# A gated filter and an MLP in fp32: the second MLP product with the weights held and a transposed output, and 97 instead of 98 positions in half of the tiles

## Chip, cores and metric

The kernel runs on one NeuronCore of one Trainium2 chip. The metric is the device time of one execution in microseconds (us). A NeuronCore has a matrix engine (TensorE, PE in the profile, with its weight loads as a row of their own, PEld), a vector engine (VectorE, DVE), a scalar engine (ScalarE, ACT), a general engine (GpSimd, POOL) and a queue engine that here only issues transfers (SyncE, SP). Each runs its own instructions in order and waits on semaphores for the others.

## What is computed

```python
def _attn_ref(x, v, pos_emb, w1, w2):            # B, S, D = 2, 12480, 128
    h_filt = (np.maximum(pos_emb @ w1, 0.0) @ w2) * np.exp(-0.01 * np.arange(S))[:, None]
    u = x * v
    L = 2 * S
    Uf = np.fft.rfft(u, n=L, axis=1)
    Hf = np.fft.rfft(h_filt, n=L, axis=0)
    y = np.fft.irfft(Uf * Hf[None, :, :], n=L, axis=1)[:, :S, :]
    return x * y

def _moe_ref(x, w_in, w_out, a, b):              # x: 24960 x 128, w_in: 128 x 2048, w_out: 2048 x 128
    h = x @ w_in
    P = a[0] + a[1] * h + a[2] * h**2 + a[3] * h**3
    Q = 1.0 + abs(b[0]) * abs(h) + abs(b[1]) * h**2
    return (P / (Q + 1e-06)) @ w_out
```

A long convolution along the sequence, a gate with x, and then an MLP with a rational activation, all in fp32.

## The kernel before

The sequence of 12480 positions is written as a grid: position = 128 m + n, with n the residue (0 to 127) and m the row (0 to 97). Residues 0 to 63 have 98 real rows, residues 64 to 127 only 97. The convolution is a Fourier transform over this grid, made of matrix products.

A first part (some 370 us) computes the filter's spectrum and the convolution of batch 0. A second part (`second_part`, taken in its `short` form) does the rest: the last Fourier step of both batches by tile (`attn_a`, `attn_b`), the MLP of every tile, and, spread between, the convolution of batch 1 (`conv_items`).

The MLP goes by 52 tiles. A tile is 5 residues of one batch (every 13th one has 4), so 5 x 98 = 490 columns (or 392) with the 128 channels on the partitions. Tiles 0 to 12 and 26 to 38 are residues from 64 up, tiles 13 to 25 and 39 to 51 residues below 64; before the change both have 98 positions a residue, the 98th of the former being a filler that isn't stored. The hidden 2048 features are done in 4 steps a tile, 4 blocks of 128 features each, so there are 208 steps. A step has two halves of two blocks:

- `mm1`: h = features x columns into PSUM, three fp32r passes a block (L870 to L872), `[128, 2, 490]` a half.
- ACT, DVE and POOL turn h into g, kept as four rows of 490 columns a step in tiles `q` and `v`: ACT writes `q` (L880, L887), `v` (L904), squares (L932, L937), takes the logarithm `l` of all four rows at once (L948) and the exponential `r` (L953); DVE does L914, L959, L964 (and L893); POOL does L969 and, last, the product `v <- v * q` (L975). A cost per row and column is so paid some 20 times a step on ACT.
- `mm2`: the second product, from `v` and `wout`, into the PSUM tile `acc`; a half is two blocks. After the 16th block `store` copies `acc` out (DVE) and SP issues the transfers.

The order of the work on each engine is written out by two strings: `FIRST` for the steps up to 94, `REST` from step 95 on. In `FIRST` each of the three slots of a step (`slot`) also issues an item of batch 1's convolution or a part of the next tile's last Fourier step, which share the one PSUM tile `cv`; in some steps POOL also multiplies a loaded piece of x and v (`uq`, L245). In `REST` the convolution is over. The order isn't touched by the change. SP issues the loads and the stores in one queue.

Of the kernel before, what the change touches and what calls it, by code (L numbers as in the profile page):

```python
# [9 lines left out]
F32 = mybir.dt.float32  # L10
# [100 lines left out]
def build(ctx: ExitStack, tc, x, x_q, v_q, pos_emb, w1, w2, w_in, w_out, moe_a, moe_b,  # L111
# [534 lines left out]
    def second_part(short):  # L646
# [142 lines left out]

        def load_xg(j):  # L790
# [36 lines left out]
        def attn_b(j):  # L827
            n = tiles[j][2]
            w = n * M
# [3 lines left out]
            def fill(cv):  # L833
                for i in range(n):
                    nc.tensor.transpose(out=cv[:, 0, i * M:(i + 1) * M], in_=t[:, i, :], identity=ident[0:M, 0:M])
# [17 lines left out]
        def width(s):  # L853
            return tiles[steps[s][0]][2] * M
# [7 lines left out]
        def mm1(s, i):  # L862
            j, c = steps[s]
            w = width(s)
            hi, lo = ah[j]
# [7 lines left out]
            st_h[s, i] = t[:, :, 0:w]  # L873
# [103 lines left out]
        def mm2(s, h):  # L977
            j, c = steps[s]
            w = width(s)
            if j not in acc:  # L980
                acc[j] = accp.tile([128, 4, D], F32, tag="acc", name="acc")
            g = st_v[s]
            for i in range(2 * h, 2 * h + 2):
                f = NWF * c + i
                for q in range(0, w, 128):
                    k = min(128, w - q)
                    nc.tensor.matmul(out=acc[j][0:k, q // 128, :], lhsT=g[:, i, q:q + k], rhs=wout[:, f, :],  # L987
                                     start=(f == 0 and q == 0), stop=(f == NF - 1), skip_group_check=True)

        def store(j):  # L990
            b, p0, n = tiles[j]
            n0 = residue(p0, n)
            w = n * M
            t = mp.tile([128, 4, D], F32, tag="ot", name="ot", bufs=2)
            a = acc.pop(j)
            nq = (w + 127) // 128
            full = w // 128
            nc.vector.tensor_copy(out=t[:, 0:full, :], in_=a[:, 0:full, :])
            if full < nq:
                k = w - full * 128  # L1000
                nc.vector.tensor_copy(out=t[0:k, full, :], in_=a[0:k, full, :])
            ob = out[b * S:(b + 1) * S, :]
            p = 0
            while p < w:
                i, m = divmod(p, M)
                k = min(M - m, 128 - p % 128)
                mm = min(k, (M if n0 + i < H2 else M - 1) - m)
                if mm > 0:
                    nc.sync.dma_start(out=ob[bass.DynSlice(m * N2 + n0 + i, mm, step=N2), :],
                                      in_=t[p % 128:p % 128 + mm, p // 128, :])  # L1010
                p += k
# [63 lines left out]
_OUTS = [((B * S, D), "float32")]  # L1075
# [30 lines left out]
```

## Time and profile before

| | |
|---|---|
| median of 3 runs | 2253.34 us (2252.31 to 2254.02) |
| profiled execution, own time | 2255.12 us |
| its span, first to last instruction | 2253.2 us |
| PE busy | 2023.2 us (90%), 13344 matmuls |
| DVE busy | 2073.7 us (92%), 2374 instructions |
| ACT busy | 1941.2 us (86%), 1971 instructions |
| POOL busy | 2021.5 us (90%), 1605 instructions |
| chain that ended last, by engine | ACT 41%, POOL 22%, PE 22%, DVE 7%, issue 5%, DMA 2% |

Busy times are averages over a first part, in which ACT has little to do, and a second part, in which four engines are nearly full. The rows of single stretches say more than the table. "The chain" is followed back from the last instruction, at each step to what released it.

### The profile page before, as it was taken

What the parts mean: (1) busy time and instruction counts of PE and PEld (TensorE: products, weight loads), DVE (VectorE), ACT (ScalarE), POOL (GpSimd) and SP (SyncE); (2) the same over time, 40 slices, a digit from 0 to 9 for tenths busy, and PEclk for the clock granted to TensorE, in tenths of its full rate; (3) what the DMA queues carried; (4) which work ended last, traced back from release to release, by engine and by line L of the source; (5) the groups of instructions that cost most, each with busy time, mean ns of one, the idle gap of its engine ahead of it and who ended that gap; (6) DMA issues with size and microseconds to landing.
All of it is one profiled execution on the core that took longest, in us unless ns stands there. A gap on an engine that the chain in (4) does not pass through costs nothing.

```text
span 2253.2 us, 35705 instructions
## 1 busy us (share of the span) xinstructions
PE 2023.2 (90%) x13344; PEld 1758.5 (78%) x13344; DVE 2073.7 (92%) x2374; ACT 1941.2 (86%) x1971; POOL 2021.5 (90%) x1605
## 2 busy tenths in 40 slices
PE   6899987899999999999999889888888898888887
PEld 4678775788888888888888777777777777777775
DVE  6899995899998998999999789999999999999996
ACT  5422224999999998999999899999999999999996
POOL 5488765999999999999999789999999999999997
PEclk9999998999999999999999999999999999999999
DMA  5344415433143233223222212212112111221100
GB/s 159 107 142 143 130 62 146 106 94 81 36 117 80 51 87 83 70 60 76 58 62 52 49 33 46 48 34 46 31 36 49 38 40 33 48 48 33 36 10 11
DMA packets 169487, 150.31 MB, mean 67 GB/s; under 512 B 91622, under 2 KB 138984, under 8 KB 166424
## 3 DMA queue, kind: packets, MB, share of 16 engines
q1 hardware_dynamic: 162280, 124.17, 22.5%
q10 hardware_dynamic: 7024, 23.76, 3.2%
q8 instruction: 107, 1.75, 0.3%
q14 instruction: 76, 0.62, 0.1%
HBM read 99.72 MB, written 48.17 MB: 66 GB/s over the span
## 4 chain that ended last, share of the span: by engine, by line
ACT 41%; POOL 22%; PE 22%; DVE 7%; issue 5%; DMA 2%; SPq 1%; POOLq 0%; DVEq 0%; ACTq 0%
POOL v L975 10%; ACT v L904 10%; ACT l L948 9%; ACT r L953 9%; PE acc L987 5%; POOL v L969 4%; ACT q L880 4%; ACT q L937 4%; ACT q L932 3%; PE cs L155 3%; PE cs L582 2%; POOL q L943 2%; PE cv L816 2%; PE h L870 1%; PE h L872 1%
## 5 line engine op out<-in xcount | busy, mean ns | idle before, releaser
L975 POOL TENSOR_TENSOR v<-v,q 128x980 f32<-128x980 f32 (+1 forms) x416 | 940.6, 2262 | 52.0 <-DVE q L964 48.7
L987 PE MATMUL acc<-wout,v 128*128 128x128 f32 (+2 forms) x6656 | 846.2, 280 | 112.4 <-POOL v L975 108.0
L987 PEld LDWEIGHTS acc<-wout,v 128*128 128x128 f32 (+2 forms) x6656 | 776.6, 187 | 191.5 <-POOL v L975 165.8
L959 DVE SCALAR_TENSOR_TENSOR q<-q,sc,r 128x980 f32<-128x980 f32 (+1 forms) x416 | 504.6, 1213 | 36.3 <-ACT r L953 34.9
L914 DVE SCALAR_TENSOR_TENSOR v<-v,sc,h 128x980 f32<-128x980 f32 (+1 forms) x416 | 504.7, 1213 | 35.4 <-ACT q L880 30.4
L964 DVE SCALAR_TENSOR_TENSOR q<-q,r 128x980 f32<-128x980 f32 (+1 forms) x416 | 482.0, 1159 | 13.5
L904 ACT ACTIVATE v<-h,sc 128x980 f32<-128x980 f32 (+1 forms) x416 | 438.1, 1082 | 30.9 <-PE h L872 29.4
L953 ACT ACTIVATE r<-l 128x980 f32<-128x980 f32 (+1 forms) x416 | 416.8, 1002 | 9.8 <-DVE q L964 8.9
L969 POOL TENSOR_SCALAR v<-v,sc 128x980 f32<-128x980 f32 (+3 forms) x321 | 422.3, 1316 | 0.0
L948 ACT ACTIVATE l<-q,sc 128x1960 f32<-128x1960 f32 (+1 forms) x208 | 401.1, 1928 | 0.7 <-POOL q L943 0.5
L870 PE MATMUL h<-ahi,win_l 128*128 128x490 f32 (+1 forms) x832 | 360.9, 434 | 28.6 <-DVE v L914 26.6
L871 PE MATMUL h<-alo,win_h 128*128 128x490 f32 (+1 forms) x832 | 319.6, 384 | 0.0
L872 PE MATMUL h<-ahi,win_h 128*128 128x490 f32 (+1 forms) x832 | 317.6, 382 | 0.0
L880 ACT ACTIVATE q<-h 128x980 f32<-128x980 f32 (+1 forms) x303 | 302.5, 998 | 8.9 <-PE h L872 8.8
L870 PEld LDWEIGHTS h<-ahi,win_l 128*128 128x128 f32 x832 | 158.6, 191 | 60.5 <-DVE v L914 38.4
L932 ACT ACTIVATE q<-q,sc 128x1960 f32<-128x1960 f32 (+1 forms) x95 | 185.9, 1957 | 0.0
L872 PEld LDWEIGHTS h<-ahi,win_h 128*128 128x128 f32 x832 | 158.0, 190 | 26.0
L937 ACT ACTIVATE q<-q,sc 128x1470 f32<-128x1470 f32 (+1 forms) x113 | 170.6, 1510 | 0.0
L871 PEld LDWEIGHTS h<-alo,win_h 128*128 128x128 f32 x832 | 159.2, 191 | 13.5 <-DVE alo L841 0.4
L816 PE MATMUL cv<-yc,gt 90*98 90x128 f32 x1004 | 127.9, 274 | 2.2 <-DVE an L822 1.0
L816 PEld LDWEIGHTS cv<-yc,gt 90*98 90x98 f32 x1004 | 118.3, 165 | 14.1 <-DVE an L822 7.5
L943 POOL TENSOR_TENSOR q<-q 128x490 f32<-128x490 f32 (+1 forms) x113 | 111.4, 986 | 9.4
(113 smaller groups left out, 2623.5 us busy)
## 6 DMA issues: line engine op xcount, KB each, us to landing
yc<-y_d SPq DMA_DIRECT2D x23, 900.0 KB
gt<-in_g_dram SPq DMA_DIRECT2D x48, 344.5 KB
xq<-in_x_q_dram SPq DMA_DIRECT2D x64, 196.0 KB
vq<-in_v_q_dram SPq DMA_DIRECT2D x64, 196.0 KB
h_d<-hg ACTq DMA_DIRECT2D x32, 360.0 KB
y_d<-ys ACTq DMA_DIRECT2D x16, 720.0 KB
hg<-h_d SPq DMA_DIRECT2D x64, 180.0 KB
y_d<-ys SPq DMA_DIRECT2D x16, 720.0 KB
```

Source lines behind the costliest of these rows:

```text
L870: nc.tensor.matmul(out=t[:, k, 0:w], lhsT=wl, rhs=hi[:, 0:w], start=True, stop=False)
L871: nc.tensor.matmul(out=t[:, k, 0:w], lhsT=wh, rhs=lo[:, 0:w], start=False, stop=False)
L872: nc.tensor.matmul(out=t[:, k, 0:w], lhsT=wh, rhs=hi[:, 0:w], start=False, stop=True)
L904: nc.scalar.activation(out=v, in_=st_h[s, i], func=AF.Square, bias=col("s"))
L914: stt(out=v, in0=v, scalar=col("k"), in1=h, op0=ALU.add, op1=ALU.mult)
L948: nc.scalar.activation(out=part(st_l, s, i), in_=part(st_q, s, i), func=AF.Ln, **({"bias": col("ka")} if short else {}))
L953: nc.scalar.activation(out=t[:, :, 0:w], in_=halves(st_l[s], i, w), func=AF.Exp, scale=-1.0)
L959: nc.vector.scalar_tensor_tensor(out=q, in0=q, scalar=col("ka") if short else 0.0, in1=st_r[s, i], op0=ALU.add, op1=ALU.mult)
L964: nc.vector.scalar_tensor_tensor(out=q, in0=q, scalar=2.0, in1=st_r.pop((s, i)), op0=ALU.subtract, op1=ALU.mult)
L969: nc.gpsimd.tensor_scalar(out=v, in0=v, scalar1=col("p0" if short else "a0"), scalar2=1.0, op0=ALU.add, op1=ALU.mult)
L975: nc.gpsimd.tensor_tensor(out=v, in0=v, in1=halves(st_q[s], i, w), op=ALU.mult)
L987: nc.tensor.matmul(out=acc[j][0:k, q // 128, :], lhsT=g[:, i, q:q + k], rhs=wout[:, f, :], start=(f == 0 and q == 0), stop=(f == NF - 1), ...
```

## The change

Three things are changed. `mm2` swaps its operands: the block of `wout` is loaded into the array as the weights and the columns of `v` stream through, one matmul a block of 485 to 490 (or 388 to 392) columns, where before pieces of 128 columns of `v` were loaded as weights and the 128 columns of `wout` streamed, four matmuls a block. `acc` is so `[channel, column]`, is copied out by one DVE instruction, and one transfer a tile writes it to an output that is laid out by channel; the host turns it round afterwards. And tiles of residues from 64 up have 97 positions a residue (`count`), so 485 or 388 columns; where fp32r matmuls or the high and low split need an even number, one more column is carried along (486).

```diff
+        def count(j):
+            return M if tiles[j][1] >= H2 else M - 1
...
         def attn_b(j):
             n = tiles[j][2]
-            w = n * M
+            k1 = count(j)
+            w = n * k1 + n * k1 % 2
...
                 for i in range(n):
-                    nc.tensor.transpose(out=cv[:, 0, i * M:(i + 1) * M], in_=t[:, i, :], identity=ident[0:M, 0:M])
+                    k = min(M, w - i * k1) if i == n - 1 else k1
+                    nc.tensor.transpose(out=cv[:, 0, i * k1:i * k1 + k], in_=t[0:k, i, :], identity=ident[0:k, 0:k])
...
         def width(s):
-            return tiles[steps[s][0]][2] * M
+            j = steps[s][0]
+            return tiles[j][2] * count(j)
...
         def mm1(s, i):
             w = width(s)
+            w += w % 2
...
         def mm2(s, h):
             if j not in acc:
-                acc[j] = accp.tile([128, 4, D], F32, tag="acc", name="acc")
-            g = st_v[s]
+                acc[j] = accp.tile([D, 512], F32, tag="acc", name="acc")
             for i in range(2 * h, 2 * h + 2):
                 f = NWF * c + i
-                for q in range(0, w, 128):
-                    k = min(128, w - q)
-                    nc.tensor.matmul(out=acc[j][0:k, q // 128, :], lhsT=g[:, i, q:q + k], rhs=wout[:, f, :],
-                                     start=(f == 0 and q == 0), stop=(f == NF - 1), skip_group_check=True)
+                nc.tensor.matmul(out=acc[j][:, 0:w], lhsT=wout[:, f, :], rhs=st_v[s][:, i, 0:w],
+                                 start=(f == 0), stop=(f == NF - 1), skip_group_check=True)

         def store(j):
-            t = mp.tile([128, 4, D], F32, tag="ot", name="ot", bufs=2)
-            nc.vector.tensor_copy(out=t[:, 0:full, :], in_=a[:, 0:full, :])
-            if full < nq:
-                nc.vector.tensor_copy(out=t[0:k, full, :], in_=a[0:k, full, :])
-            while p < w:
...
-                    nc.sync.dma_start(out=ob[bass.DynSlice(m * N2 + n0 + i, mm, step=N2), :],
-                                      in_=t[p % 128:p % 128 + mm, p // 128, :])
+            w = n * count(j)
+            t = mp.tile([D, NPT * M], F32, tag="ot", name="ot", bufs=2)
+            nc.vector.tensor_copy(out=t[:, 0:w], in_=acc.pop(j)[:, 0:w])
+            r0 = n0 * M - max(0, n0 - H2)
+            nc.sync.dma_start(out=out[b, :, r0:r0 + w], in_=t[:, 0:w])
```

On PE, in the last `FIRST` step that begins before the 4-residue tile of batch 0, a half of the second product (`acc`) stands between a convolution item (L215) and the next (L155), with the first product of the 4-residue tile (`h`, 128x392) behind. The sizes are partitions x columns of what is written. Before:

```order
L215 MATMUL cv<-idfth,yy 90x2x64 x4
L987 MATMUL acc<-wout,v 128x128 x3
L987 MATMUL acc<-wout,v 106x128
L987 MATMUL acc<-wout,v 128x128 x3
L987 MATMUL acc<-wout,v 106x128
L155 MATMUL cv<-f_66,uq_5084 128x180 x2
L870 MATMUL h<-ahi,win_l 128x392
```

And at the same place after the change:

```order
L215 MATMUL cv<-idfth,yy 90x2x64 x4
L992 MATMUL acc<-v,wout 128x485 x2
L155 MATMUL cv<-f_66,uq_4774 128x180 x2
L878 MATMUL h<-ahi,win_l 128x388
L879 MATMUL h<-alo,win_h 128x388
```

Eight matmuls with 128 streamed columns each have become two with 485; nothing was moved past anything else.

On SP, the store of a tile stands between the loads for a later tile (`xt`, `gt`, `yc`) and those of the convolution (`hg`). Before:

```order
L143 DMA xt<-in_x_dram 96x640
L146 DMA xt<-in_x_dram 2x640
L797 DMA gt<-in_g_dram 90x980
L779 DMA yc<-y_d_64 90x32x80
L1009 DMA out_dram<-ot 97x128
L1009 DMA out_dram<-ot 30x128
L1009 DMA out_dram<-ot 67x128
L1009 DMA out_dram<-ot 60x128
L1009 DMA out_dram<-ot 37x128
L1009 DMA out_dram<-ot 90x128
L1009 DMA out_dram<-ot 7x128
```

And after:

```order
L146 DMA xt<-in_x_dram 2x640
L801 DMA gt<-in_g_dram 90x980
L779 DMA yc<-y_d_64 90x32x80
L1002 DMA out_dram<-ot 128x485
L703 DMA hg<-h_d 128x2x180
L692 DMA y_d_65<-ys 90x2048
```

Eight transfers (an eighth row, 97x128, follows those shown) have become one, in the same place of the queue.

## Rows read from the trace of the kernel before

**Rows 1.** Busy time by stretch: us, then PE, PEld, DVE, ACT, POOL, granted clock, DMA.
```profile
600.00:800.00 200.00, 190.55 (x1355) 174.84 (x1353) 186.16 (x186) 197.25 (x182) 194.98 (x164) 1.00 0.32 78
2000.00:2200.00 200.00, 173.91 (x1179) 150.03 (x1179) 195.94 (x204) 199.85 (x192) 198.00 (x143) 1.00 0.14 31
```

**Rows 2.** Waits of ACT, 420 to 2253 us: total, times, longest.
```profile
ACT v L904 <- PE h L872: 18.3, 19, 3.7
```

**Rows 3.** Timeline, two FIRST steps: start, duration, engine, line.
```profile
717.78 1.96 ACT L948 ACTIVATE l<-q,sc 128x1960 f32<-128x1960 f32 x1
...
727.37 1.98 ACT L948 ACTIVATE l<-q,sc 128x1960 f32<-128x1960 f32 x1
...
735.36 0.38 PE L872 MATMUL h<-ahi,win_h 128*128 128x490 f32 x1
...
735.78 1.08 ACT L904 ACTIVATE v<-h,sc 128x980 f32<-128x980 f32 x1
...
736.75 1.93 ACT L948 ACTIVATE l<-q,sc 128x1960 f32<-128x1960 f32 x1
```

**Rows 4.** Timeline of ACT, a FIRST step without a convolution item on ACT.
```profile
803.70 1.99 ACT L948 ACTIVATE l<-q,sc 128x1960 f32<-128x1960 f32 x1
...
812.81 2.01 ACT L948 ACTIVATE l<-q,sc 128x1960 f32<-128x1960 f32 x1
```

**Rows 5.** Groups by form: tiles of 5 and of 4 residues (count, busy, mean ns).
```profile
L975 POOL TENSOR_TENSOR v<-v,q 128x980 f32<-128x980 f32 x384 | 880.8, 2295 | 45.0 <-DVE q L964 41.7 <-ACT q L932 3.1
...
L948 ACT ACTIVATE l<-q,sc 128x1960 f32<-128x1960 f32 x192 | 375.3, 1955 | 0.2
...
L975 POOL TENSOR_TENSOR v<-v,q 128x784 f32<-128x784 f32 x32 | 59.8, 1868 | 7.0 <-DVE q L964 7.0
...
L948 ACT ACTIVATE l<-q,sc 128x1568 f32<-128x1568 f32 x16 | 25.8, 1612 | 0.5 <-POOL q L943 0.5
```

**Rows 6.** The chain, 726 to 734 us: start, time on the chain, what.
```profile
726.12 1.77 PE acc L987 x16
...
733.20 0.31 PE cv L190 x2
...
```

**Rows 7.** Timeline of PE and its weight loads, first product.
```profile
729.27 0.38 PE L871 MATMUL h<-alo,win_h 128*128 128x490 f32 x1
729.49 0.38 PE L872 MATMUL h<-ahi,win_h 128*128 128x490 f32 x1
```
**Rows 8.** Timeline of the weight loads alone, same stretch.
```profile
729.27 0.19 PEld L872 LDWEIGHTS h<-ahi,win_h 128*128 128x128 f32 x1
```

**Rows 9.** The chain in REST: POOL's second product of a step, twice.
```profile
1704.72 2.27 POOL v L975
...
1713.10 2.28 POOL v L975
```

**Rows 10.** Timeline of ACT in REST, start of the l of steps 107 and 108.
```profile
1400.37 1.97 ACT L948 ACTIVATE l<-q,sc 128x1960 f32<-128x1960 f32 x1
1408.66 2.00 ACT L948 ACTIVATE l<-q,sc 128x1960 f32<-128x1960 f32 x1
```

**Rows 11.** Timeline of ACT, l of a tile of 4 residues (steps 152 and 155).
```profile
1776.61 1.61 ACT L948 ACTIVATE l<-q,sc 128x1568 f32<-128x1568 f32 x1 [0.18 <-POOL q L943]
...
1801.02 1.60 ACT L948 ACTIVATE l<-q,sc 128x1568 f32<-128x1568 f32 x1
```

**Rows 12.** The chain in the same stretch.
```profile
1789.95 2.16 PE acc L987 x16
```

**Rows 13.** Timeline of POOL after the 4-residue tile of batch 0 in FIRST.
```profile
889.02 2.30 POOL L975 TENSOR_TENSOR v<-v,q 128x980 f32<-128x980 f32 x1 [2.01 <-ACT q L932]
```

**Rows 14.** Timeline of the end of the kernel.
```profile
2242.63 2.43 PE L987 MATMUL acc<-wout,v 128*128 128x128 f32 x16 [0.56 <-POOL v L975]
2245.10 0.56 DVE L998 COPY ot<-acc 128x384 f32<-128x384 f32 x1 [4.51 <-PE acc L987]
2245.68 3.44 SPq L1009 DMA_DIRECT2D out_dram<-ot  x7
```

More of the change, by code (lines that the diff above doesn't have):

```diff
@@ L872, in mm1 @@
                 nc.tensor.matmul(out=t[:, k, 0:w], lhsT=wh, rhs=hi[:, 0:w], start=False, stop=True)
-            st_h[s, i] = t[:, :, 0:w]
+            st_h[s, i] = t[:, :, 0:width(s)]
         def act_q(s, i):
@@ L992, in store @@
             n0 = residue(p0, n)
-            w = n * M
-            t = mp.tile([128, 4, D], F32, tag="ot", name="ot", bufs=2)
-            a = acc.pop(j)
-            nq = (w + 127) // 128
-            full = w // 128
-            nc.vector.tensor_copy(out=t[:, 0:full, :], in_=a[:, 0:full, :])
-            if full < nq:
-                k = w - full * 128
-                nc.vector.tensor_copy(out=t[0:k, full, :], in_=a[0:k, full, :])
-            ob = out[b * S:(b + 1) * S, :]
-            p = 0
-            while p < w:
[L1005 to L1008, printed above, removed]
-                    nc.sync.dma_start(out=ob[bass.DynSlice(m * N2 + n0 + i, mm, step=N2), :],
-                                      in_=t[p % 128:p % 128 + mm, p // 128, :])
-                p += k
+            w = n * count(j)
[3 more added lines that the diff above has]
+            nc.sync.dma_start(out=out[b, :, r0:r0 + w], in_=t[:, 0:w])
         at = []
@@ L1074, with by_position @@
 _INS = ["x", "v", "pos_emb", "w1", "w2", "moe_w_in", "moe_w_out", "moe_a", "moe_b"]
-_OUTS = [((B * S, D), "float32")]
+_OUTS = [((B, D, S), "float32")]
+def by_position(a):
+    a = a.reshape(B, D, S).transpose(0, 2, 1)
+    r = np.empty((B, S, D), np.float32)
+    o = 0
+    for n in range(N2):
+        k = M if n < H2 else M - 1
+        r[:, n::N2] = a[:, o:o + k]
+        o += k
+    return r.reshape(B * S, D)
 def by_quarter(x):
@@ L1104 @@
     r = _run(nc, [arrays], core_ids=[0])
-    return r.results[0]["out_0_dram"]
+    return by_position(np.asarray(r.results[0]["out_0_dram"]))
```

## The prediction

> **What bounds the kernel now.** I read the busy time by stretch first. The second part has two stretches: while the convolution of batch 1 runs (`FIRST`) ACT is busy 197.25 of 200 us, PE 190.55 and POOL 194.98; after it (`REST`) ACT 199.85, POOL 198.00, DVE 195.94, and PE only 173.91, always with the full granted clock [rows 1]. So PE isn't what limits most of the time, and a cheaper second product is worth only what it frees the others from. Then the starts of ACT's `l`, which comes once a step: 9.59 us apart in a `FIRST` step with a convolution item on ACT, 9.11 us in one without, and between two starts ACT's instructions follow each other without a gap [rows 3, 4]. But of the 95 steps up to the switch, 14 that have no such item take 9.36 to 9.41 us; one of them is 727.37 to 736.75, in which ACT's `v` at 735.78 begins when the first product's last pass has just ended (735.36 plus 0.38) [rows 3]. There PE is late by 9.38 - 9.11 = 0.27 us, and the chain of what ended last runs over PE for 12 us ahead of it, with two halves of the second product in it [rows 6]. In all ACT's `v` waits 18.3 us for the first product, 19 times that the list counts [rows 2]. In `REST` the chain goes round in POOL (a second product `v * q` every 8.38 us) or in ACT (8.29 us), two loops that are equal within 1% [rows 9, 10].
>
> **The second product.** Before, a half takes 1.77 us on the chain: 16 records, two for each of 8 matmuls of 128 streamed columns, so 0.111 us a record [rows 6]. What streaming 485 columns costs is bounded by the same kind of matmul with 180 columns: two records in 0.31 us, 0.155 each, that is 0.86 ns a column [rows 6]; from the two sizes, (0.155 - 0.111) / 52 gives 0.85 ns a column and next to nothing fixed. A record of 485 columns is then 0.41 us, a half (four records) 1.63 to 1.65 us, with 490 columns 1.65 to 1.67, with 388 or 392 1.32 to 1.34. I take 0.13 us a half off, since 512 streamed columns become 485 to 490 and nothing else is saved. In a tile of 4 residues a half took 2.16 us on the chain [rows 12] (its last piece of 8 columns is streamed against all 128 columns too), and there 0.83 us goes.
>
> The weight load must be hidden for this. In the first product a load of 128 columns (0.19 us) starts with the pass ahead of it and the passes follow each other by 0.22 us, for 490 columns in fp32r [rows 7, 8], so the load lies under the pass. The Trainium skill has a rule that speaks against it: "TensorE: Matmul & The Clock Gate", in Part 3 under "What overlaps and what doesn't", says that weight loads overlap with running matmuls only where they go to other rows of the array, and these loads fill all of them. By that rule each of the four loads of a half would stand in line with the passes; it is the rival on the other side below. The passes of the first product do not follow it.
>
> What the 0.13 us is worth:
> - *`FIRST`, tiles of 5 residues.* PE is late by 0.27 us in 14 steps, and about two halves lie on the chain ahead of each [rows 3, 6]: 2 x 0.13 = 0.26 us, so nearly all of it goes: 14 x 0.24 = **3.3 us**. Bounds: 0 and 3.8.
> - *The 4-residue tile in `FIRST`* (steps 48 to 51). PE and POOL are both full there, since POOL also multiplies a loaded piece in each step. PE shortened doesn't help while POOL is full; what it does help is the gap of 2.01 us that POOL has behind it, waiting for ACT, that is for PE [rows 13]: **2.0 us**, bounds 0 and 5.
> - *The 4-residue tiles in `REST`* (steps 100 to 103 and 152 to 155). The last three intervals of such a tile take 24.41 us, 8.14 each [rows 11], with the chain on PE. The ACT loop would need 8.29 less 18 rows of 98 columns at 0.875 ns, so 6.75 us; the POOL loop 8.38 less 0.85 us for `v * q` alone, so 7.5 at most [rows 5, 9, 10]. That is 1.9 to 4.2 us a tile; PE gives back 4 x 0.83 = 3.3. I take 2.5, twice: **5.0 us**, bounds 3 and 7.
>
> **The 97 positions.** In steps 0 to 51 and 104 to 155 a row has 485 columns for 490. From the forms for 5 and 4 residues, a column costs 0.875 ns on ACT ((1955 - 1612) / 392) and 2.18 ns on POOL's product ((2295 - 1868) / 196) [rows 5]; I take ACT's price for all of ACT's forms. A `FIRST` step has 20 rows on ACT, so 100 columns or 0.087 us less. ACT is what limits there, and 48 such steps give **4.2 us**. In `REST` ACT has 18 rows, 0.079 us less, and POOL at least 4 x 5 x 2.18 = 0.044 us less, with its other forms a little more; the slower loop is POOL's, so 0.06 us in each of 48 steps: **2.9 us**. No row of this case has an odd number of columns, nor four separate rows of odd length; the 4-residue forms are strided and pay nothing for it (their fixed share is the same). Bounded below by no extra cost (nothing suggests a gain), above by each row being rounded up to the next 16 columns, 496: then narrow tiles are no gain, and the POOL loop loses 4 x 6 x 2.18 = 0.05 us. I take the lower bound, to which 392 columns in strides are nearest.
>
> **The copy and the stores.** One copy of 485 columns takes the place of two, and one transfer that of eight, in the same places on DVE and SP. Both are off the path in the steady state: the next tile's accumulation waits for the copy, as before, and loads queued behind the store on SP are wanted a tile later; the cover is a tile's 33 to 38 us. At the end nothing covers them. The last half of the second product (2.43 us from 2242.63) becomes about 1.6, and from the start of the copy at 2245.10 the kernel runs to 2253.2: seven issues take 3.44 us, 0.49 each, and the rest is the landing of the last [rows 14]. With one issue 2.9 us go. The landing is of 200 KB at once, spread over 128 long rows, for a last piece of at most 49 KB: unknown, between 2 us less and 2 us more; I take the same. The end so gives 0.8 + 2.9, rounded with the second copy's part to **4.0 us**, bounds 1 and 6.
>
> **Sum.** 3.3 + 2.0 + 5.0 + 4.2 + 2.9 + 4.0 = 21.4 us. The profiled execution took 2255.1 us for a span of 2253.2, and the median of the runs is 1.8 us below it: 2253.3 - 21.4 = 2231.9, so **2232 us**, 0.95% faster.
>
> **Rivals.**
> 1. *More than that.* The kernel recovers from every disturbance (a burst of `uq`, a late load) at PE's pace, and the list has 18.3 us of ACT waiting for PE of which I count only a part [rows 2]. With the upper bounds of the second product's three terms (15.8 for 10.3) and of the end (6), the time is 2224. For it: PE is the only engine that gets slack; against: POOL has 97% in `FIRST` [rows 1].
> 2. *The second product gives nothing back in `FIRST`.* POOL takes over where PE was late: only the narrow tiles, the `REST` tiles and the end remain, 16.1 us, less with their lower bounds (3 and 1): 2237 to 2242. For it: POOL's 194.98 of 200 [rows 1].
> 3. *Odd rows cost.* By the upper bound above 4.2 + 2.9 go and 2.4 us come on top (48 x 0.05): 11.9 us are left, 2241. For it: POOL's loop has no slack in `REST` [rows 9]; against: no fixed cost of strides [rows 5].
> 4. *The other side: the weight load isn't hidden* under the fp32 passes. Four loads a half at 0.11 us (the pace of records that carried one 128-column load each [rows 6]) make 1.65 into 2.1 us, 0.3 more than before. In `FIRST` PE has no slack over two steps [rows 3], so of the 2 x 0.3 us a step nearly all shows: 79 steps with convolution and 5 residues give some 40 us more, against 16 us from the rest: about 2277. It decides from a half of 1.8 us up. Against it: [rows 7, 8].
> 5. *It changes nothing that counts,* because the three full engines trade waits: 2249 to 2257.
>
> **How the numbers follow.** Chances: the forecast (2226 to 2236) 0.5, more (1) 0.13, nothing back in `FIRST` (2) 0.15, odd rows (3) 0.11, weight load (4) 0.06, no change (5) 0.05. I leave out (4) and (5) and part of the tails: 2217 to 2243. A change of 0.2%, 4.5 us, is about what a measurement of this kernel can tell from none. Faster by more: the first four, 0.89; within it 0.05; slower 0.06.
>
> **What would show it.** A half of `mm2` at 1.63 to 1.67 us with four records, its weight loads under the passes; `l` 9.50 us apart in narrow `FIRST` steps and 9.59 in wide ones, without steps of 9.38 in the wide ones; 8.2 to 8.35 in narrow `REST` steps; 4-residue tiles at 7.0 to 7.5 us a step; the end some 4 us shorter behind the last `v * q`. Wrong would be: `v * q` of 485 columns no shorter than 2295 ns, a half above 1.8 us, or ACT waiting for POOL where it waited for PE.

## The result and the profile after

Before, the median of four runs was 2253.68 us (2252.31 to 2255.26); after it, 2228.53 us (2226.01 to 2229.54). The ratio is 0.9884, with a 95% interval of 0.9871 to 0.9897: faster by 1.16%, 25.2 us, for a forecast of 2232. The profiled execution of after took 2228.3 us for a span of 2226.4, so between the two profiled spans there are 26.8 us.

The stretches of [rows 1] again, now of the changed kernel (busy us and instructions of PE, PEld, DVE, ACT, POOL, then granted clock, DMA share, GB/s):

```profile
600.00:800.00 200.00, 187.05 (x864) 131.09 (x863) 185.95 (x183) 197.54 (x184) 195.71 (x167) 1.00 0.31 78
2000.00:2200.00 200.00, 167.97 (x604) 98.96 (x604) 192.85 (x196) 198.38 (x193) 198.00 (x145) 1.00 0.09 23
```

PE is 3.5 to 6 us emptier in 200, while ACT and POOL are as full as before within 1.5 us. ACT's wait for the first product, 18.3 us in [rows 2], over the same part of the run (list of waits: total, times, longest):

```profile
ACT v L912 <- PE h L880: 8.0, 8, 2.3
```

A half of the second product, in the timeline of PE, first in `FIRST` with 5 residues, then in `REST` with 4. In this view the duration runs to the modelled end of the last record, 0.16 to 0.17 us past the start of PE's next work, to which the chain counts:

```profile
731.39 1.79 PE L992 MATMUL acc<-v,wout 128*128 128x485 f32 x4
733.01 0.59 PE L841 MATMUL cv<-ident,an 97*128 97x97 f32 x5
...
1345.12 1.48 PE L992 MATMUL acc<-v,wout 128*128 128x392 f32 x4
```

The last two of its four weight loads, in the timeline of the loads:

```profile
731.79 0.19 PEld L992 LDWEIGHTS acc<-v,wout 128*128 128x128 f32 x1 [0.22 <-issue]
732.20 0.19 PEld L992 LDWEIGHTS acc<-v,wout 128*128 128x128 f32 x1 [0.22 <-issue]
```

The half begins at 731.39 and the next work of PE at 733.01: 1.62 us for four records of 485 columns, as forecast. Both loads run inside it, beside a pass of the same half, and the half is no longer for them.

ACT's `l`, once a step, in the timeline of ACT: a narrow `FIRST` step, a wide one without an item on ACT, a 4-residue step in `REST`, and a narrow `REST` step:

```profile
807.88 2.05 ACT L956 ACTIVATE l<-q,sc 128x1940 f32<-128x1940 f32 x1
817.40 2.06 ACT L956 ACTIVATE l<-q,sc 128x1940 f32<-128x1940 f32 x1
...
1024.43 2.06 ACT L956 ACTIVATE l<-q,sc 128x1960 f32<-128x1960 f32 x1
1033.61 2.03 ACT L956 ACTIVATE l<-q,sc 128x1960 f32<-128x1960 f32 x1
...
1343.33 1.61 ACT L956 ACTIVATE l<-q,sc 128x1568 f32<-128x1568 f32 x1
1350.53 1.60 ACT L956 ACTIVATE l<-q,sc 128x1568 f32<-128x1568 f32 x1
...
1399.55 1.92 ACT L956 ACTIVATE l<-q,sc 128x1940 f32<-128x1940 f32 x1
1407.79 1.94 ACT L956 ACTIVATE l<-q,sc 128x1940 f32<-128x1940 f32 x1
```

So a narrow `FIRST` step takes 9.52 to 9.53 us instead of 9.59 to 9.60, a late wide one about 9.2 instead of 9.38 [rows 3], a 4-residue step in `REST` 7.20 instead of 8.78 (the like step of before, 1358.39 to 1367.17), and a narrow `REST` step 8.24 instead of 8.30.

To see where the 26.8 us came from, the span is cut at the starts of the 208 `l`s (step 0 is the first). These are differences of starts, in us; the last three columns belong to experiments below.

| steps | before | after | change | `held_98` | `only_97` | `before_4x98` |
|---|---|---|---|---|---|---|
| start to 6 | 437.84 | 436.80 | -1.04 | 438.64 | 438.59 | 438.02 |
| 6 to 48, narrow, `FIRST` | 402.61 | 398.53 | -4.08 | 401.18 | 399.61 | 401.84 |
| 48 to 54, 4 residues and what follows | 61.10 | 56.04 | -5.06 | 56.14 | 61.05 | 57.05 |
| 54 to 89, wide, `FIRST` | 333.59 | 332.09 | -1.50 | 332.13 | 333.60 | 333.60 |
| 89 to 99, the switch to `REST` | 100.10 | 97.22 | -2.88 | 98.33 | 98.28 | 99.87 |
| 99 to 104, 4 residues | 40.19 | 37.46 | -2.73 | 38.49 | 40.18 | 38.15 |
| 104 to 151, narrow, `REST` | 393.02 | 390.13 | -2.89 | 393.59 | 390.67 | 393.05 |
| 151 to 156, 4 residues | 40.83 | 39.05 | -1.78 | 38.07 | 40.66 | 38.72 |
| 156 to 203, wide, `REST` | 393.08 | 393.00 | -0.08 | 393.05 | 393.03 | 393.00 |
| 203 to the end | 50.84 | 46.08 | -4.76 | 45.98 | 50.53 | 48.90 |

Wide steps in `REST`, which have as many columns as before and in which PE isn't late, are the control: they don't change. The part up to step 6 differs by as much between kernels that are equal there, so it is no gain of the change. A segment's noise is up to 0.8 us: steps 6 to 48 take 399.61 us in `only_97` and 400.41 in `old_97_4x98` below, which do the same work there.

### The profile page after: what moved, and what is told of

Same layout as the page of the kernel before. It is cut to its first block, busy times and chain, and to the rows that moved or that the text cites. A ratio compares the mean times of both kernels' runs of the same rounds, so it can differ in the third digit from the quotient of the medians.

```text
span 2226.4 us, 25191 instructions
## 1 busy us (share of the span) xinstructions
PE 1951.9 (88%) x8352; PEld 1307.8 (59%) x8352; DVE 2060.4 (93%) x2322; ACT 1932.1 (87%) x1971; POOL 2014.7 (90%) x1605
## 4 chain that ended last, share of the span: by engine, by line
POOL 37%; ACT 36%; DVE 10%; PE 9%; issue 5%; DMA 2%; SPq 0%; POOLq 0%; DVEq 0%; ACTq 0%
POOL v L983 18%; POOL v L977 8%; ACT v L912 8%; ACT r L961 8%; ACT l L956 7%; ACT q L940 6%; ACT q L888 5%; POOL q L951 4%; POOL q L950 2%; PE cs L155 2%; PE cs L582 2%; DVE q L967 2%; DVE q L972 1%; ACT q L945 1%; DVE v L922 1%
## 5 line engine op out<-in xcount | busy, mean ns | idle before, releaser
L983 POOL TENSOR_TENSOR v<-v,q 128x970 f32<-128x970 f32 (+3 forms) x416 | 936.3, 2252 | 42.5 <-DVE q L972 40.9
L992 PE MATMUL acc<-v,wout 128*128 128x485 f32 (+3 forms) x1664 | 765.9, 583 | 123.9 <-POOL v L983 116.9
L922 DVE SCALAR_TENSOR_TENSOR v<-v,sc,h 128x970 f32<-128x970 f32 (+3 forms) x416 | 502.9, 1209 | 36.7 <-ACT q L888 32.3
L967 DVE SCALAR_TENSOR_TENSOR q<-q,sc,r 128x970 f32<-128x970 f32 (+3 forms) x416 | 502.6, 1208 | 36.9 <-ACT r L961 34.0
L972 DVE SCALAR_TENSOR_TENSOR q<-q,r 128x970 f32<-128x970 f32 (+3 forms) x416 | 480.1, 1154 | 13.4
L912 ACT ACTIVATE v<-h,sc 128x970 f32<-128x970 f32 (+3 forms) x416 | 445.3, 1105 | 19.5 <-PE h L880 19.2
L961 ACT ACTIVATE r<-l 128x970 f32<-128x970 f32 (+3 forms) x416 | 426.0, 1024 | 8.7 <-DVE q L972 7.9
L878 PE MATMUL h<-ahi,win_l 128*128 128x486 f32 (+3 forms) x832 | 391.7, 471 | 47.2 <-DVE v L922 45.4
L977 POOL TENSOR_SCALAR v<-v,sc 128x980 f32<-128x980 f32 (+6 forms) x321 | 420.8, 1311 | 0.1
L956 ACT ACTIVATE l<-q,sc 128x1940 f32<-128x1940 f32 (+3 forms) x208 | 405.3, 1949 | 2.2 <-POOL q L951 2.1
```

What stands on the lines that cost most here:

```text
L878: nc.tensor.matmul(out=t[:, k, 0:w], lhsT=wl, rhs=hi[:, 0:w], start=True, stop=False)
L912: nc.scalar.activation(out=v, in_=st_h[s, i], func=AF.Square, bias=col("s"))
L922: stt(out=v, in0=v, scalar=col("k"), in1=h, op0=ALU.add, op1=ALU.mult)
L956: nc.scalar.activation(out=part(st_l, s, i), in_=part(st_q, s, i), func=AF.Ln, **({"bias": col("ka")} if short else {}))
L961: nc.scalar.activation(out=t[:, :, 0:w], in_=halves(st_l[s], i, w), func=AF.Exp, scale=-1.0)
L967: nc.vector.scalar_tensor_tensor(out=q, in0=q, scalar=col("ka") if short else 0.0, in1=st_r[s, i], op0=ALU.add, op1=ALU.mult)
```

## Experiments

Each kernel was timed beside runs of the kernel before on the same chip. A ratio's interval is about 0.17% to either side, so two experiments that lie less than 4 us apart are told apart by the segments of their profiles rather than by their times.

**Weights held, 98 positions.** The narrow tiles keep the padding position through both products; the store leaves it out.

```diff
         def count(j):
-            return M if tiles[j][1] >= H2 else M - 1
+            return M
```

> The second product with the weights held and the new output, but 98 positions a residue in every tile. Theory: the 97 positions alone are worth 0.06 us in each of 96 steps of five residues, about 6 us (read from the two traces), so 6 us above the changed kernel: 2234 to 2235. Rival: rows of 485 are no cheaper and the time is that of the changed kernel, 2228 to 2230. Rival: most of the gain hangs on the narrower tiles, then above 2240.

Measured 2235.9 us (2234.18 to 2239.25), ratio 0.992 [0.9903, 0.9936]: within 1 us of the theory's range and below the second rival's.

**97 positions alone.** The kernel before with the tiles of 97 positions; the second product still takes `v` as the weights, and the stores go by row.

> The second product and the stores of before, with 97 positions a residue in tiles of residues from 64 up. Theory: the two parts are nearly additive, 5 to 7 us below before: 2246 to 2249. Rival: with the second product of before the narrow steps are held by PE and give nothing back: 2252 to 2254.

Measured 2247.96 us (2246.55 to 2249.87), ratio 0.9974 [0.9964, 0.9985], in the theory's range. So the 97 positions are worth 5.9 us alone and 7.4 with the weights held, equal within the intervals, and the rest of the change 17.9 alone. In the table the two hardly meet: 97 positions act in the narrow tiles, the rest in tiles of 4 residues, at the end, and in the `FIRST` steps in which PE was late.

**More streamed columns, by an extra matmul.** A second matmul for each block streams the missing columns. Its start flag comes after the first one's, and the sum then lacks block 0: the output is off by 0.249 of its size, where one missing block of 16 would make a quarter.

```diff
                 nc.tensor.matmul(out=acc[j][:, 0:w], lhsT=wout[:, f, :], rhs=st_v[s][:, i, 0:w], ...)
+                nc.tensor.matmul(out=acc[j][:, w:512], lhsT=wout[:, f, :], rhs=st_v[s][:, i, 0:512 - w], ...)
```

> The changed kernel with one more matmul a block that streams the first 512 - w columns of v once more into the unused columns of acc (they are never read), so that 512 columns are streamed a block as before the change, in tiles of four residues too. Theory: what PE gets back is the streamed columns, so the 0.2 us stalls in FIRST, the catching up behind the four-residue tiles and the transition at step 95 come back in part: 2236 to 2242. Rival: what counted was fewer matmuls and weight loads or the new output: 2228 to 2232.

Measured 2248.39 us (2245.04 to 2249.5), ratio 0.9971 [0.9958, 0.9983], 6 us above the worst expectation. The edit did something else than it was meant to. The timeline of PE in this kernel, one half:

```profile
699.65 0.98 PE L992 MATMUL acc<-v,wout 128*128 128x485 f32 x2
700.46 0.30 PE L994 MATMUL acc<-v,wout 128*128 128x27 f32 x2
700.60 1.06 PE L992 MATMUL acc<-v,wout 128*128 128x485 f32 x2
701.50 0.30 PE L994 MATMUL acc<-v,wout 128*128 128x27 f32 x2
701.64 0.61 PE L841 MATMUL cv<-ident,an 97*128 97x97 f32 x5
```

From 699.65 to 701.64 the half takes 1.99 us where 512 columns in one piece would take 1.74: two records of 27 columns take 0.14 us, and the two of 485 behind them 0.90 where the first two take 0.81. A pass of 27 columns too short to lie over the next load of 0.19 us would explain both; no run varies its length. So this is not the test of streamed columns, but a test of a half that is too long. Steps 6 to 48 take 405.43 us and steps 54 to 89 338.75, 6.9 and 6.7 more than after.

**More streamed columns, in one piece.** Each matmul streams two overlapping rows of 256 columns; the copy takes the two parts that make a whole row.

```diff
+                a = st_v[s][:, i, 0:256]
+                two = bass.AP(a.tensor, a.offset, [list(a.ap[0]), [w - 256, 2], [1, 256]])
-                nc.tensor.matmul(out=acc[j][:, 0:w], lhsT=wout[:, f, :], rhs=st_v[s][:, i, 0:w], ...)
+                nc.tensor.matmul(out=acc[j].rearrange("p (k w) -> p k w", k=2), lhsT=wout[:, f, :], rhs=two, ...)
```

> The changed kernel, but each matmul of the second product streams two overlapping rows of 256 columns, 512 in all instead of 485 to 490 (388 to 392 in a tile of 4 residues); weights held, four records and two loads a pair as in the change, the result the same. Theory (the columns streamed are what the change saves on PE): a half rises from 1.65 to about 1.74 us, PE is late again, narrow steps without an item on ACT go from 9.1 back to 9.2 or 9.3, the 4-residue tiles lose most of what they won, and of the 15 us that the weights held gave before the end of the run, 9 to 15 go back: 2237 to 2243. Rival (the fewer records, loads and PSUM openings are what saves): 2228 to 2232.

Measured 2231.67 us (2230.68 to 2232.2), ratio 0.9899 [0.9882, 0.9916]. The timeline of PE, a half of 5 residues in `FIRST` (one of 4 in `REST` shows 1.88):

```profile
729.05 1.89 PE L994 MATMUL acc<-v,wout 128*128 128x512 f32 x4
```

The half has its length from the theory (0.16 less on the chain, so 1.72), but only 3 us go back, not 9 to 15: 1.1 in steps 6 to 48, 0.7 in 48 to 54, 0.5 in 54 to 89, 0.5 in 99 to 104. The theory falls in its size: by the times, the columns that the change saves are a small part of its gain. (In the `FIRST` steps in which PE was late they are half of it; see the table of these steps below.) Most of it must lie in what this kernel still shares with the change.

**Sixteen records again, weights held.** The same 512 columns, cut into four matmuls of 128 a block; two copies make a whole row of them.

```diff
+                for k in range(4):
+                    q = min(128 * k, w - 128)
+                    nc.tensor.matmul(out=acc[j][:, 128 * k:128 * k + 128], lhsT=wout[:, f, :],
+                                     rhs=st_v[s][:, i, q:q + 128], ...)
```

> The changed kernel, but each block's matmul is cut into four of 128 streamed columns with the same held weights (the fourth begins 128 columns ahead of the row's end), so 16 records and 16 weight loads a half as before the change; the result is the same. Streaming 512 columns in one piece cost 3 us over the change (2231.7). Theory (only the length of a half counts, and 16 records of 0.111 us make 1.78 in every tile, against 1.72 in one piece and 2.26 before in a tile of 4 residues): 2231 to 2235, with the 4-residue tiles still some 4 us shorter in FIRST than before. Rival (the number of loads and records is what costs PE, whatever it holds): most of the gain ahead of the end goes, 2240 to 2246. Third (weights loaded from v, which POOL has only just written, are what costs): as the theory, but with halves below 1.7 us.

Measured 2236.25 us (2236.12 to 2239.63), ratio 0.9927 [0.9911, 0.9944], just above the theory's range and below the rival's. Timeline of PE, a half of 5 residues and one of 4:

```profile
730.49 1.95 PE L994 MATMUL acc<-v,wout 128*128 128x128 f32 x16
...
1356.12 1.95 PE L994 MATMUL acc<-v,wout 128*128 128x128 f32 x16
```

With 5 residues that is what the old product takes as well (1.94 in the kernel before). With 4 residues it is not: there the kernel before has, in the same view,

```profile
1360.67 2.33 PE L987 MATMUL acc<-wout,v 128*128 128x128 f32 x16
```

Sixteen records of 128 streamed columns each, and 0.38 us longer. Two things set the old product apart there: its fourth piece has 8 columns of weights (392 = 3 x 128 + 8), where a tile of 5 residues has 106, and its rows of 392 are stored 490 apart.

**The old product without the piece of 8.** In 4-residue tiles the kernel before takes one piece of 98 columns for each residue; the store follows (four transfers for seven).

```diff
+                e = M if tiles[j][2] == 4 else 128
-                for q in range(0, w, 128):
-                    k = min(128, w - q)
+                for q in range(0, w, e):
+                    k = min(e, w - q)
```

> The kernel before, but in tiles of 4 residues the pieces are four of 98 columns instead of 128, 128, 128 and 8, one for each residue, so four stores instead of seven. Theory (the piece of 8 columns is what makes a half 2.26 us there instead of 1.78): a half 1.78 us, steps 48 to 53 some 3 to 4 us shorter, each 4-residue tile in REST 1.5 to 2 us shorter, the end 2 us shorter (0.4 from the half, 1.5 from three issues): 2242 to 2246. Rival (rows of 392 columns, 490 apart, make the loads from v slow there): only the end is shorter, 2250 to 2253. Third (POOL is full in steps 48 to 53): only REST and the end, 2245 to 2249.

Measured 2243.12 us (2241.35 to 2244.11), ratio 0.995 [0.9934, 0.9967]: 9.8 us faster than before, the theory's range. The half in a 4-residue tile, timeline of PE:

```profile
1362.05 1.91 PE L988 MATMUL acc<-wout,v 128*98 128x128 f32 x16
```

It is 0.42 us shorter than with the piece of 8, with as many records and streamed columns, and the same rows of v. The weight loads of the two halves show where the time goes, first in the kernel before (the half from 1360.67), then here:

```profile
1360.57 0.97 PEld L987 LDWEIGHTS acc<-wout,v 128*128 128x128 f32 x8
1361.75 0.96 PEld L987 LDWEIGHTS acc<-wout,v 128*128 128x128 f32 x8 [0.22 <-issue]
1362.93 0.19 PEld L870 LDWEIGHTS h<-ahi,win_l 128*128 128x128 f32 x1 [0.22 <-DVE an L822]
```

```profile
1361.84 1.91 PEld L988 LDWEIGHTS acc<-wout,v 128*98 128x98 f32 x16
```

With the piece of 8, whose two loads are the last of a block's eight, no load runs for 0.22 us behind each of the two blocks, 0.44 a half; with four pieces of 98 all sixteen follow each other. In 4-residue tiles of 97 positions `only_97` has a last piece of 4 columns, and the half shows 2.32 us there as well.

In the 4-residue tiles of the table this kernel wins most of what the change wins or more (4.05 of 5.06, 2.04 of 2.73, 2.11 of 1.78), at the end 1.94 of 4.76, three issues fewer included, and elsewhere at most 0.77, which is the noise of a segment.

**Both by the old product.** 97 positions and pieces by residue, weights still from v, stores by row.

> The kernel before with two edits at once: 97 positions a residue in narrow tiles (2247.96 by itself) and, in tiles of 4 residues, one piece for each residue (2243.12 by itself); the second product still takes v as weights and the stores are by row. Theory (the two add up, since one shortens ACT's and POOL's rows and the other PE's halves in three tiles and the end): 9.8 + 5.9 = 15.7 us off, 2235 to 2239 against a before of about 2253, so that what is the weights' holding and the output by channel is worth 8 to 10 us of the change's 25. Rival (they win the same time, since with shorter rows ACT is held up by POOL instead): 2240 to 2243.

Measured 2239.09 us (2238.09 to 2240.09), ratio 0.9934 [0.9917, 0.995]: 14.6 us, where the two alone give 15.7. They add up within the interval.

**Half the columns.** In 14 of 16 blocks only 256 columns are multiplied, so the sum lacks those blocks in the other columns.

```diff
+                k = w if f in (0, NF - 1) else 256
-                nc.tensor.matmul(out=acc[j][:, 0:w], lhsT=wout[:, f, :], rhs=st_v[s][:, i, 0:w], ...)
+                nc.tensor.matmul(out=acc[j][:, 0:k], lhsT=wout[:, f, :], rhs=st_v[s][:, i, 0:k], ...)
```

> The changed kernel, but in 14 of the 16 blocks of a tile only the first 256 columns are multiplied, so the sum lacks those blocks in the other columns; it measures what still more slack on PE is worth. A half falls from 1.65 to about 0.9 us. Theory (after the change PE is hardly ever what comes last; ACT and POOL are): steps with full tiles stay at 9.53 and 9.59, 8.24 and 8.30, and only the 4-residue steps and the end give 1 to 4 us: 2224 to 2228. Rival (bursts are still made up at PE's pace): as much again as the change gave in FIRST, 8 to 15 us: 2213 to 2220. Third: PE idles more, its granted clock falls in places, and the time is that of the change or 1 to 5 us longer: 2228 to 2234.

Measured 2237.01 us (2232.38 to 2239.64), ratio 0.9928 [0.9911, 0.9945]: less work on PE, and some 4 to 11 us more than after. It goes the third way and beyond it. Two windows of this kernel, columns as above:

```profile
1400.00:1600.00 200.00, 151.18 (x630) 105.03 (x628) 193.97 (x198) 198.36 (x193) 196.69 (x144) 0.96 0.16 38
1890.00:1892.50 2.50, 1.75 (x4) 1.18 (x4) 2.47 (x3) 2.50 (x3) 2.50 (x3) 0.53 0.00 0
```

Two halves of four records of 256 columns in the timeline of PE, both behind a wait for POOL, the second in the second window:

```profile
1416.29 1.13 PE L993 MATMUL acc<-v,wout 128*128 128x256 f32 x4 [0.86 <-POOL v L983]
...
1890.75 2.08 PE L993 MATMUL acc<-v,wout 128*128 128x256 f32 x4 [1.19 <-POOL v L983]
```

Four such records are 0.87 us by 0.85 ns a column, and 0.86 in `FIRST` (719.45 to 720.31); where the granted clock is 0.53 the half takes nearly twice as long. Wide steps in `REST`, the control, take 397.30 us for 393.00, about as much more as the whole profiled execution (a span of 2230.4 for 2226.4). There ACT's `v` waits for PE again, which it never does in these steps of after (waits of ACT, 1789 to 2185 us):

```profile
ACT v L912 <- PE h L880: 3.6, 8, 0.6
```

In steps 6 to 48 it is 1.35 us faster than after, so there was little more to win from PE in `FIRST`: ACT and POOL set the pace.

**The store in eight column transfers.**

```diff
-            nc.sync.dma_start(out=out[b, :, r0:r0 + w], in_=t[:, 0:w])
+            cut = [w * k // 8 for k in range(9)]
+            for c0, c1 in zip(cut, cut[1:]):
+                nc.sync.dma_start(out=out[b, :, r0 + c0:r0 + c1], in_=t[:, c0:c1])
```

> The changed kernel with each store cut into eight transfers of some 61 columns. Theory: only the end of the kernel sees it, seven issues of 0.3 to 0.5 us: 2230.5 to 2232. Rival: the eight issues also hold up loads on the SP queue in the steady state and at step 95: 2233 or more.

Measured 2236.2 us (2234.7 to 2237.31), ratio 0.9922 [0.9905, 0.9938]: 7.7 us above after, more than expected. Up to step 203 the profile is 0.7 us longer than after's, with no segment more than 1.3 us away; the end is 6.3 longer. Timeline of its end, span 2233.4:

```profile
2221.17 0.57 DVE L1000 COPY ot<-acc 128x392 f32<-128x392 f32 x1 [3.66 <-PE acc L992]
2221.76 5.32 SPq L1004 DMA_DIRECT2D out_dram<-ot  x8
```

The eight issues take 5.32 us, 0.67 each, and 6.3 us pass from the end of the last to the end of the run (2233.4 - 2227.08), where after needs 4.0. So the issues cost more than the 0.49 us each that the prediction read from the kernel before, and the landing is longer too; whether by the short rows of a piece or by the number of transfers isn't shown. In the steady state the stores show no cost.

**Rows without gaps.** `q`, `v` and `l` are stored with a pitch of their own width, 485, 392 or 388 for 490.

```diff
-            return mp.tile([128, k, NPT * M], F32, tag=tag, name=tag, bufs=bufs)
+            t = mp.tile([128, k * NPT * M], F32, tag=tag, name=tag, bufs=bufs)
+            return t[:, 0:k * w].rearrange("p (k w) -> p k w", k=k)
```

> The changed kernel with the rows of q, v and l stored one behind the other in narrow and 4-residue tiles (485, 392 and 388 columns apart instead of 490), so that a form of 2 to 4 rows is one run of elements on each engine. Theory (the rows with gaps between them cost ACT some 7 ns a form, which is why 20 columns less gave 10 ns and not 17): ACT's l goes from 1.81 to 1.80 us from start to start, a narrow FIRST step from 9.53 to 9.50, and the time is 1 to 2 us shorter: 2226.5 to 2228. Rival (gaps cost nothing, the odd number of columns does): no change, 2228 to 2229.5. Third (rows that begin at odd addresses cost POOL or DVE something): 2230 or more.

Measured 2226.79 us (2225.57 to 2228.79), ratio 0.9877 [0.9861, 0.9894], the best of all by its median, though its runs overlap with those of after. Two `l`s in the timeline of ACT:

```profile
808.49 2.01 ACT L957 ACTIVATE l<-q,sc 128x1940 f32<-128x1940 f32 x1
818.00 2.02 ACT L957 ACTIVATE l<-q,sc 128x1940 f32<-128x1940 f32 x1
```

A narrow `FIRST` step takes 9.51, for 9.52 to 9.53 after. From the start of `l` to the next start on ACT, over 38 steps, the mean is 1.804 us for 1.810. The theory holds in the trace, at 6 ns a form (`flat_2q`, stored in the same way, has 1.804 too), and is below what the times can tell.

**An even number of columns.** 486 in the elementwise work and the second product, the last one a dummy; the first product had 486 already.

> The changed kernel with 486 columns in the elementwise work and both products of a narrow tile instead of 485, the last of them a dummy; the output is unchanged. Theory (odd rows cost): the forms of 485 columns lose a fixed charge, narrow FIRST steps go from 9.53 to 9.51 or less, POOL's v * q stays at 2272 ns or falls, 2227 to 2228.5. Rival (one column more is one column more): v * q 2276 ns, a step 0.01 to 0.02 us longer, 2228.5 to 2230.

Measured 2231.71 us (2226.51 to 2233.17), ratio 0.9897 [0.9879, 0.9915]; no gain. POOL's `v * q` of 972 columns takes 2280 ns, for 2272 with 970, and the narrow step 9.54 for 9.53. The rival holds: one column more is one column more. All runs have an even number of columns in the first product, so what an odd one would do there isn't shown.

**The last store on two queues**, with rows without gaps: 64 channels on SP, 64 on ACT.

> The rows of q, v and l stored without gaps, as in the run of that name (2226.8), and the last tile's store cut into two halves of 64 channels, one issued by SP and one by ACT. Theory (the landing of 200 KB depends on its size): from the copy's start to the end 3.0 to 4.3 us instead of 4.95, 2225 to 2226.5. Rival (the landing is a fixed time): no change, 2226 to 2228.5.

Measured 2228.96 us (2227.08 to 2232.68), ratio 0.9887 [0.9871, 0.9904]. Timeline of its end, span 2230.7:

```profile
2224.52 0.57 DVE L1001 COPY ot<-acc 128x392 f32<-128x392 f32 x1 [3.65 <-PE acc L993]
2225.11 0.57 SPq L1004 DMA_DIRECT2D out_dram<-ot  x1
2225.11 0.58 ACTq L1005 DMA_DIRECT2D out_dram<-ot  x1
```

From the issue to the end 5.6 us, for 4.35 with one transfer in after. The theory falls: half the bytes on each of two queues landed no earlier.

## Why the prediction held, and where its sum was wrong

The forecast's direction, its size and most of its steps held. One term was wrong by its argument (the 4-residue tile in `FIRST`, 3.1 us too small), one gain had no term (the switch, 2.9), one was too large (the 97 positions in `FIRST`, 1.2), and one explanation was wrong. What the sum lacked is as much as the whole 6 us from the forecast to the lower end of its range, and the term that was too large took some of it back: that the time lies well inside is partly luck.

*The second product's half.* Predicted 1.63 to 1.65 us, measured 1.62 to 1.65. The loads lie under fp32 passes; the rival of exposed loads (4) is refuted for passes of 388 columns and more. The rule of the Trainium skill that stood beside it ("TensorE: Matmul & The Clock Gate", Part 3, "What overlaps and what doesn't") is not what this trace shows: loads of 128 columns over all 128 rows (0.19 us) run inside a pass that uses the same rows. Behind passes of 27 columns the half does get longer. The price that I put on that rival was too high, too: with halves of 1.99 us the kernel is still 0.3% faster than before, where I let it lose from 1.8 us up. Against `only_97`, whose halves take 1.78, it loses 5.8 us in steps 6 to 48 and 5.2 in 54 to 89, of 2 x 0.21 us in 77 steps, 32 us. Of these 11.0 us 8.4 are in the 14 steps in which PE was late before; in the others PE has the slack.

*`FIRST`, 5 residues.* 3.3 us forecast, for 14 steps in which PE was late (12, 16, 20, 24, 36, 40 and 56 to 84 by fours). These steps can be followed by the length of a half, from PE's start to its next work:

| kernel | half, us | the 14 steps, us | mean |
|---|---|---|---|
| `stream_512` | 1.99 | 139.63 | 9.97 |
| before | 1.78 | 131.31 | 9.38 |
| `only_97` | 1.78 | 131.28 | 9.38 |
| `pieces_128` | 1.78 | 131.39 | 9.39 |
| `overlap_512` | 1.72 | 129.67 | 9.26 |
| `held_98` | 1.65 | 128.52 | 9.18 |
| after | 1.62 to 1.65 | 128.09 | 9.15 |
| `stream_256` | 0.86, at a tile's ends more | 127.49 | 9.11 |

So 3.2 us come of it, and the mechanism is as forecast: the steps follow the half's length, down to the 9.11 us of a step that ACT sets. Holding the weights alone gives nothing (`pieces_128`). About half of the 3.2 comes of fewer streamed columns (after against `overlap_512`), the other half of one piece in place of four.

*The 4-residue tile in `FIRST`.* 2.0 forecast, 5.06 measured; this is the step that failed, and by its argument: "PE shortened doesn't help while POOL is full". POOL behaves as I said. Its gap of 2.01 us [rows 13] is gone, and its own instructions take as long as before: the timeline of POOL after has the last product of the tile and the first of the next without a gap, in one line (x2).

```profile
879.96 4.15 POOL L983 TENSOR_TENSOR v<-v,q 128x776 f32<-128x776 f32 x2
...
886.95 2.34 POOL L983 TENSOR_TENSOR v<-v,q 128x980 f32<-128x980 f32 x1
```

But the buffers between ACT and POOL let ACT run ahead. At step 51 POOL's first `v * q` starts 11.20 us behind the `l` of its step (874.09 and 862.89), for 8.14 before (879.23 and 871.09); at step 56 it is 6.94, for 7.00. ACT went ahead by 3 us while POOL was full, and POOL, which further on in wide `FIRST` steps is busy only 187.60 of 200 us (1000 to 1200), made it up within 5 steps, where ACT sets the pace. A full engine is a limit only for as long as its backlog isn't worked off in slack behind it.

*The 4-residue tiles in `REST`.* 5.0 forecast, 2.73 + 1.78 = 4.5 measured. The second falls short by the clock. Windows of after, columns as above, then the like stretch of `store_8`, which does the same work on PE there:

```profile
1755.00:1760.00 5.00, 3.20 (x10) 1.72 (x9) 4.93 (x7) 4.46 (x6) 4.92 (x5) 0.90 0.00 0
1760.00:1765.00 5.00, 5.00 (x15) 3.15 (x14) 2.81 (x4) 3.10 (x5) 4.92 (x5) 0.76 0.00 0
```

```profile
1756.00:1761.00 5.00, 3.20 (x13) 1.94 (x11) 4.93 (x7) 4.45 (x6) 4.92 (x5) 1.00 0.00 0
```

The granted clock has two levels, 2.4 GHz (1.00) and 1.2 (0.50); 0.90 and 0.76 are means over both. PE idled 1.8 of the 5 us up to 1760 and then ran part of the time at the lower level; the step from 1756.36 took 9.14 us. In `store_8` PE idled as long, the clock stayed, and the step took 7.73. So the fall is no mark of the change: of five profiled executions with this work on PE, or one column more, it comes here in two (after and `flat_rows`, 9.14 and 9.11 us) and not in `store_8`, `even_486` and `flat_2q` (7.72 to 7.73); `flat_2q` has one in the first tile instead (9.08). It costs 1.4 us; without it the tiles give some 5.7. `held_98` has the same in the first tile (9.06 for 7.92).

*Why these tiles gave so much* was explained wrongly. I wrote that "its last piece of 8 columns is streamed against all 128 columns too". So is a piece of 106, and 16 records at 0.111 us would be 1.78, not 2.16. That the half was longer with the same number of records needed a cause of its own. `before_4x98` shows it: a half of 1.91 for 2.33 in the timeline, and 9.8 us in all, fewer stores at the end included, without weights held or an output by channel. The loads show a pause of 0.22 us behind each short pair; why it comes is not settled. The record of a load of 8 columns is 87 ns, shorter than the others. No run tried pieces between 8 and 98.

*97 positions.* 4.2 + 2.9 forecast. In steps 6 to 48, after against `held_98` shows 2.65 in 42 steps, 0.063 a step for 0.087; over 48 steps that is 3.0. In `REST` it is 2.9 in 47 steps between before and after, as forecast (2.35 between before and `only_97`, 3.46 between `held_98` and after). By the times it is 5.9 to 7.4. Odd rows (3) show no cost (`even_486`); rows apart cost ACT some 6 ns a form (`flat_rows`), a part of what is missing (20 columns less took 11 ns off `l`, 1.821 to 1.810, for the 17 priced). POOL's product behaved as priced, 22 ns for 10 columns. Groups by form, after (count, busy, mean ns, idle before):

```profile
L983 POOL TENSOR_TENSOR v<-v,q 128x980 f32<-128x980 f32 x192 | 440.5, 2294 | 26.2 <-DVE q L972 25.9
L983 POOL TENSOR_TENSOR v<-v,q 128x970 f32<-128x970 f32 x192 | 436.0, 2272 | 14.1 <-DVE q L972 12.8 <-ACT q L940 0.9
```

*The end.* 4.0 forecast, 4.76 measured from step 203. The rows that answer to [rows 14], with the window before them:

```profile
2214.00:2220.00 6.00, 5.39 (x9) 2.64 (x10) 2.62 (x3) 0.83 (x1) 5.11 (x4) 0.52 0.01 4
```

```profile
2221.46 0.57 DVE L1000 COPY ot<-acc 128x392 f32<-128x392 f32 x1 [3.84 <-PE acc L992]
2222.05 0.33 SPq L1002 DMA_DIRECT2D out_dram<-ot  x1
```

From the copy's start to the end 4.9 us for 8.1; after the last issue 4.0, for 4.1 with small pieces, so the landing is the same, which I chose between 2 less and 2 more. The last halves run in part at the lower clock here; in `held_98` and `store_8`, with 1.00 and 0.96 there, the last half takes 1.58 us in the timeline, the 1.6 of the forecast.

*Not foreseen: the switch to `REST`*, 2.88 us, in steps 94 and 96. There PE runs at a lower granted clock in places before and after: from 1305 to 1315 before, 0.66, with a half of 3.41 us on the chain; after, the like stretch has

```profile
1290.00:1300.00 10.00, 6.43 (x22) 4.23 (x20) 9.44 (x11) 10.00 (x11) 6.75 (x5) 0.83 0.35 50
```

and no such half. Step 96 takes 9.00 to 9.08 us in all four kernels with the old product and 8.30 to 8.72 in those with the weights held and halves up to 1.78. Step 94 takes 20.0 to 20.2 us in three of the four and 17.7 to 19.0 in the others, but 18.31 in `only_97`, the fourth, where the granted clock over this step was 1.00 for 0.83 before. `old_97_4x98`, with the same 97 positions, gains nothing at the switch (100.12 us), so they alone don't win it; which edit moves the falls of the clock stays open.

*No rival took the place of the forecast.* "More" (1) was the nearest: 2228.5 lies halfway to its 2224, by the 4-residue tile in `FIRST` and by the switch, which it didn't name. "Nothing back in `FIRST`" (2) and "odd rows" (3) would have ended 8 to 13 us higher.

Put by causes, from the times: 9.8 us are the piece of 8 columns with the stores that go with it, 5.9 the 97 positions (14.6 together), and 10.6 are left for weights held and the output by channel (2239.09 to 2228.53). From kernel to kernel these are 2.8 to `pieces_128` (1.6 of it at the end, 48.12 to 46.54 us from step 203), 4.6 more to `overlap_512` for one piece in place of four, and 3.1 more for the columns, each a step about as large as its interval.

## What to carry to other kernels

Where a tile's stage takes longer than the count of its instructions explains, find that out before the change that removes it is priced: here a tail of 8 weight columns cost some 10 us in three tiles and the end, and cutting the tile by residue would have got that with a few lines. A full engine off the pace-setting one isn't a wall: look at how many buffers lie between the two and whether there is slack behind the full stretch. And taking ever more work off PE was no gain here: with halves of 0.86 us the kernel was slower than with 1.62 to 1.65.

## What the runs showed that was not expected

- The granted clock was lower where PE had less to do: 1.00 in 1400 to 1600 us after (PE busy 172.29 of 200), 0.96 with 256 columns (151.18), and single halves of that kernel take 2.08 us in the timeline for 1.13. A single fall isn't tied to the program: with the same work on PE it came in some executions and not in others.
- A half with pieces of 8 weight columns takes longer than one with pieces of 106, 2.33 and 1.94 us, with 16 records each, and no load runs for 0.22 us behind each block's short ones.
- Four records of 27 columns make a half 0.36 us longer (1.99 for 1.63) for 108 columns, which by 0.85 ns a column are 0.09.
- A store of 196 KB lands 4.0 us after its issue in one transfer, and no earlier in two on two queues (5.6 from issue to end, for 4.35); cut into eight by columns, it takes 11.6 from the first issue.
